# Where the weight transposes of a two-block transformer run, forward and backward on one core: DMA in the opening, TensorE between two passes

## The chip, the cores and the metric

The program runs on one core of a Trainium2 chip. The metric is the device time of one launch in microseconds (us). A core has five instruction streams that each run in order: TensorE (PE, matmuls and the transposes it can do against an identity), VectorE (DVE), ScalarE (ACT), GpSimd (POOL) and SyncE (SP). Here DMAs are issued from two of these streams, SP and ACT; their data move on 16 DMA engines that the two share.

## The reference, cut to what matters

Four layers A, B, A, B on x of 2048 x 640, with weights shared between the two A layers and between the two B layers, and then all gradients. Heads: 32 of width 20.

```python
x = x + A(layernorm(x))   # linear attention
x = x + B(layernorm(x))   # softmax attention over a window of 256
x = x + A(layernorm(x))
x = x + B(layernorm(x))
# A: q, k, v = h @ wqkv; phi(t) = where(t > 0, t + 1, exp(t)) + 1e-6
#    kv = sum_s phi(k) v;  z = sum_s phi(k);  o = phi(q) kv / (phi(q) z);  return o @ wo
# B: o = softmax(mask(q k^T / sqrt(20))) v;  return o @ wo
out, vjp = jax.vjp(f, A_x, A_wqkv, A_wo, B_wqkv, B_wo)
return (out, *vjp(grad_out))
```

The backward pass multiplies by the transposed weights, so each of the four weight matrices is needed once as it is and once transposed. Those four transposes are what the change moves.

## The kernel before, in words

x is cut into 16 tiles of 128 rows (TT = 16), the width into 5 blocks of 128 (DT = 5). `forward` runs four stages one after the other, and the stages overlap only at their seams.

1. The opening: `a_first` for layer 0. Per tile: `ln` (lines 469 to 484: two BATCH_NORM_STATS2 and the aggregate on DVE, two small activations on ACT for the reciprocal root, one DVE operation that writes `hn`), a transpose of `hn` on PE with an ACT copy, a store of `hn` from SP (line 484), and six chunks of q, k, v (`a_qkv`, five matmuls of 320 columns each), with their exponentials on ACT and their maxima on DVE; ACT issues five stores per tile. `hn` has one buffer (`hnA`, line 372), so the `hn` of a tile waits until the store of the tile before has landed.
2. Pass 0 (`ab_pass(0)`): for each tile the second half of layer 0 (`a_num`, `out_proj`), all of layer 1 (`ln`, `b_qkv`, `attn`, `out_proj`) and the first half of layer 2.
3. Between the passes: the key-value sums of layer 2 (`a_kv(2)`) and six tiles of late queries (`late_q`), which are fillers for PE.
4. Pass 2: the second half of layer 2, all of layer 3, and the first steps of the backward pass.

After `forward` come four backward stages, which read the transposed weights from DRAM (`WqTA`, `WoTA`, `WqTB`, `WoTB`).

What sets the order inside `forward` is a planner (`Sched`, line 87). Every step is recorded as an `Op` with an engine, a duration or a DMA size, and the buffers it reads and writes. `Sched.order` (line 126) then plays the program through with its own costs (lines 164 to 178), always taking the operation that can start first, and the instructions are emitted in that order; each engine executes its own in order. In the planner's book a DMA transpose ("T") holds SP for about 1.26 us and a shared channel for 1.17 us per 160 KB; a plain DMA ("D") holds SP for 0.33 us. A filler is taken only if nothing else can start within 300 ns (line 160). The planner's dependencies shape the order only; the waits in the program come from the buffers that the instructions touch. The framework also gives each DMA, from SP or ACT alike, one of eight completion counters in turn (they show as DMAHW0 to DMAHW7 among the waits in the built program), and an issue waits until the DMA that had the counter before has landed.

Weight transposes before the change:

- `wflips` (line 906): 20 pairs, spread by `wf` and `ws` (line 958) over pass 0. Each pair is a DMA transpose of a 128 x 640 block of `Wqkv_A` (15) or `Wo_A` (5) from SBUF into a `pp` buffer (two of them), issued by SP, and a store of that buffer to `WqTA` or `WoTA`, also from SP.
- `bflips` (line 919): 15 such pairs between the passes, from `B_wqkv` in DRAM into `KT`, `QT` and `e` buffers and out to `WqTB`.
- `early_dO` (line 712): at the start of pass 2, five DMA transposes of `Wo_B` into `WoTB` (which lies over `vv`, so after the last reader of layer 2's v), and one store.

Loads and zeroing before: lines 936 to 938 issue x in three parts (tile 0; tiles 1 to 3; tiles 4 to 15). Lines 1041 to 1044 load `Wo_A`, `Wqkv_B` and `Wo_B` in 15 pieces; they name ("vv", tt, 5) as what they follow, which at that point of the recording has no writer yet, so that they follow nothing. Lines 1039 to 1040 put 14 memsets on DVE that zero `mbd` and the q, k, v slabs of layer 1; they have no predecessor either. In PSUM the score banks of `attn` (`s3`, three banks, and `s1`) are the tiles `singles`.

Of the kernel before, what the change touches and what calls it, by code (L numbers as in the profile page):

```python
# [86 lines left out]
class Sched:  # L87
# [38 lines left out]
    def order(self):  # L126
# [23 lines left out]
        while len(out) < len(self.ops):  # L150
# [16 lines left out]
            if o.dma:  # L167
                kind, size = o.dma
                if kind == "T":
# [31 lines left out]
class Kern:  # L201
# [130 lines left out]
    def forward(self, slabs):  # L332
# [5 lines left out]
        with ExitStack() as st:  # L338
# [130 lines left out]
            def ln(l, tt, hn, hnT, how):  # L469
# [14 lines left out]
                dma("SP", lambda: self.tm_view(self.hn_d[l])[:, tt, :], lambda: hn.t, 160 * KB, [hn], [])  # L484
# [421 lines left out]
            def wflips(i, gate):  # L906
                def f():
                    et, part = divmod(i, 4)
                    key, dst, n, a = ("Wqkv_A", "WqTA", self.QTT, part * DT) if part < 3 else ("Wo_A", "WoTA", DT, 0)
                    c0 = part * D if part < 3 else 0  # L910
                    b = R["pp"].buf()
                    keys = [("Wqkv_A", i) for i in range(6)] if part < 3 else [key]
                    view = lambda: b.t.rearrange("p (k q) -> p k q", k=DT)
                    flip(view, lambda: wsb[key][:, et, c0:c0 + D], 160 * KB, keys + [gate], [b])
                    dma("SP", lambda: W[dst].rearrange("p (a b) -> p a b", a=n)[:, a:a + DT, et * P:(et + 1) * P],
                        view, 160 * KB, [b], [])
                return f

            def bflips(i, gate):
                def f():  # L920
                    et, part = divmod(i, 3)
                    kind = ("KT", "QT", "KT", "e", "e")[i % 5]
                    b = R[kind].buf()
                    view = lambda: (b.t[:, 0:DT, :] if kind != "e" else
                                    b.t.rearrange("p h i q -> p (h i) q")[:, 0:DT, :])
                    flip(view, lambda: self.B_wqkv[et * P:(et + 1) * P, part * D:(part + 1) * D], 160 * KB, [gate], [b])
                    dma("SP", lambda: W["WqTB"].rearrange("p (a b) -> p a b", a=self.QTT)[
                        :, part * DT:(part + 1) * DT, et * P:(et + 1) * P], view, 160 * KB, [b], [])
                return f
# [28 lines left out]
            AT = {0: dict(wf=-2.296, ws=0.65, num=-2.458, out=-1.707, outb=1.792, step=0.144, qkv=-0.99, wide=0.745, lag=0.42, af=2.042, al=-0.11),  # L958
                  2: dict(lq=-3.207, num=-2.403, out=-1.76, outb=1.696, step=0.086, qkv=-0.985, wide=0.584, lag=0.35, gT=0.745, dO=1.691, dOs=0.137)}

            def ab_pass(l, last):
# [75 lines left out]
            a_first(items, 0, 0)  # L1037
            spread(items, 1.0, 9.0, [lambda f=f: op("POOL", 350, f, [], ["masks"]) for f in self.mask_steps])
            spread(items, 2.0, 12.0, [lambda t=t, v=v, n=n: op("DVE", 100 + n * 0.45, lambda: nc.vector.memset(t, v), [],
                                                               ["zeros"]) for t, v, n in zeros])  # L1040
# [7 lines left out]
            for i in range(3 * DT):  # L1048
                bflips(i, ("rs", 1, TT - 1))()
            for tt in range(EARLY):  # L1050
# [3 lines left out]
                        for o in S.rd.get(k, ())}  # L1054
            a_users = {o for i in range(6) for o in S.rd.get(("Wqkv_A", i), ())}
# [812 lines left out]
```

## Time and profile before

| what | us |
|---|---|
| device time, median of 3 runs (lowest, highest) | 2163.03 (2159.4, 2163.52) |
| the profiled execution's own device time | 2163.08 |
| its span, first to last instruction | 2161.4 |
| the opening, to the last transpose of `pqT` | 0 to about 113 |
| pass 0, first product with `mbd` to the last scores | about 118 to 418 |
| between the passes, to the second product with `mbd` | about 418 to 452 |
| mean granted TensorE clock | 0.973 |

How to read the lines: in a timeline the columns are start, duration, engine, line, operation, out<-in, how many were merged, and in brackets how long the engine had been idle and what released it. SPq and ACTq are DMA issues on these streams. In a view of stretches each engine has its busy time and its number of instructions, then the granted PE clock (1.00 is full), the busy share of the 16 DMA engines and GB/s. In a list of DMA issues the last two columns are KB of one and the median us from issue to landing. Matmul ends are modelled, so a group's start-to-start distance says more than its duration.

### The profile page before, as it was taken

Reading aid. Unit: us, or ns where it says so; the run is one execution under the profiler, and the core shown is the slowest. Engines: PE = TensorE matmul, PEld = TensorE weight load, DVE = VectorE, ACT = ScalarE, POOL = GpSimd, SP = SyncE. Lnnn points to the kernel's source line nnn. Section 1 sums busy time; section 2 is a strip of 40 time slices with the busy share of each in tenths; the row PEclk is TensorE's granted clock in tenths of the full one; section 3 lists DMA queues with packets and bytes.
Section 4 is the critical chain, followed back from the end, with each engine's and each line's share of the span. In section 5 each row is a group of like instructions: output and inputs, shape, how many; then the busy total and the mean of one; then the engine's idle time right before and its main releaser. Section 6 shows DMA issues by size and latency. Waiting matters only on the chain. (4 is left out here: it accounts for less than half of the span.)

```text
span 2161.4 us, 67833 instructions
## 1 busy us (share of the span) xinstructions
PE 2008.5 (93%) x27808; PEld 1384.3 (64%) x27808; DVE 1441.9 (67%) x2954; ACT 1191.9 (55%) x1975; POOL 879.2 (41%) x1850
## 2 busy tenths in 40 slices
PE   6878899879999899999899999998999999999999
PEld 4645666556666567777666667655777765666764
DVE  7656677567777489999734459605999984444651
ACT  4617778617888589899522223215889882121430
POOL 1015566506777556666323213203656651221210
PEclk9979999999999989999999999998999989999999
DMA  7449998788999688988997899836998997989843
GB/s 274 171 136 194 191 199 185 173 220 182 211 210 199 144 157 157 159 155 151 200 187 168 208 196 214 181 95 143 154 159 151 166 169 162 195 181 230 186 112 102
DMA packets 964808, 379.70 MB, mean 176 GB/s; under 512 B 844817, under 2 KB 944785, under 8 KB 964241
## 3 DMA queue, kind: packets, MB, share of 16 engines
q1 hardware_dynamic: 887296, 302.44, 72.5%
q10 hardware_dynamic: 77200, 72.94, 10.9%
q8 instruction: 217, 3.56, 0.7%
q14 instruction: 95, 0.77, 0.1%
HBM read 109.02 MB, written 112.07 MB: 102 GB/s over the span
## 5 line engine op out<-in xcount | busy, mean ns | idle before, releaser
L1668 DVE TENSOR_TENSOR ds_sb<-pair,e_sb 128x768 bf16<-128x768 f32 x480 | 438.0, 952 | 58.4 <-PE pair L1629 50.9
L1648 ACT ACTIVATE e_sb<-pair 128x768 bf16<-128x768 f32 x480 | 391.0, 815 | 95.6 <-PE pair L1629 66.3
L841 POOL TENSOR_SCALAR_AFFINE_SELECT e_sb<-e_sb 128x384 bf16<-128x384 bf16 (+1 forms) x512 | 198.2, 406 | 373.7 <-ACT e_sb L832 347.3
L832 ACT ACTIVATE e_sb<-s_ps 128x1152 bf16<-128x1152 f32 (+2 forms) x256 | 273.9, 1070 | 107.0 <-PE s_ps L828 71.0
L1660 POOL TENSOR_SCALAR_AFFINE_SELECT e_sb<-e_sb 128x256 bf16<-128x256 bf16 x448 | 182.1, 407 | 226.9 <-ACT e_sb L1648 226.8
L1302 POOL TENSOR_TENSOR gw<-w,gcar 128x640 f32<-128x640 f32 x64 | 89.4, 1398 | 423.9 <-ACT w L1299 400.4
L1113 PEld LDWEIGHTS <-slabR 128*128 128x128 bf16 x1920 | 185.7, 98 | 116.2 <-DMA slabR<-o 5.8
L1657 POOL TENSOR_SCALAR_AFFINE_SELECT e_sb<-e_sb 128x256 bf16<-128x256 bf16 x512 | 206.5, 406 | 90.1 <-ACT e_sb L1648 90.1
L1693 PEld LDWEIGHTS <-dsT 128*128 128x128 bf16 x2880 | 146.3, 97 | 96.7 <-issue 90.4
L1684 ACT COPY dsT<-dsT_ps 128x768 bf16<-128x768 bf16 x240 | 191.2, 797 | 10.2 <-PE dsT_ps L1681 7.3
L446 PE MATMUL mm_ps<-slabR,hnTB 128*128 128x320 bf16 x960 | 170.5, 309 | 8.4 <-DVE gcar L518 6.1
L1681 PE MATMUL dsT_ps<-ident,ds_sb 128*128 128x128 bf16 x1848 | 158.4, 223 | 1.6 <-ACT dsT L1684 1.1
L1697 PEld LDWEIGHTS <-e_sb 128*128 128x128 bf16 x2880 | 145.2, 96 | 0.0
L1697 PEld LDWEIGHTS <-ds_sb 128*128 128x128 bf16 x2880 | 145.1, 96 | 0.0
L846 POOL TENSOR_SCALAR_AFFINE_SELECT e_sb<-e_sb 128x512 bf16<-128x512 bf16 x224 | 142.5, 636 | 0.0
L835 ACT ACTIVATE e_sb<-s_ps 128x384 bf16<-128x384 f32 (+2 forms) x256 | 119.8, 468 | 36.6 <-PE s_ps L828 10.1
L1113 PE MATMUL dw_ps<-dqkv,slabR 128*128 128x480 bf16 x640 | 134.6, 366 | 0.0
L1113 PE MATMUL dw_ps<-dqkv,om 128*128 128x480 bf16 x640 | 134.2, 366 | 0.0
L1284 ACT ACTIVATE dh<-mm_ps 128x320 f32<-128x320 f32 x64 | 28.0, 437 | 191.6 <-PE mm_ps L1113 153.3
L1629 PE MATMUL pair<-slabR 32*128 32x384 bf16 (+2 forms) x1024 | 121.6, 329 | 11.5 <-DVE ds_sb L1668 5.0
L866 PE MATMUL pv_ps<-v_slab,e_sb 128*128 128x32 bf16 x2880 | 117.7, 177 | 12.9 <-POOL e_sb L846 10.7
L866 PEld LDWEIGHTS <-e_sb 128*128 128x128 bf16 x2880 | 106.0, 96 | 35.6 <-POOL e_sb L846 14.6
(227 smaller groups left out, 4299.3 us busy)
## 6 DMA issues: line engine op xcount, KB each, us to landing
qkvp<-qk_slab SPq DMA_DIRECT2D x64, 256.0 KB, 3.4
hn<-slabR SPq DMA_DIRECT2D x64, 160.0 KB, 3.0
qkvp<-v_slab SPq DMA_DIRECT2D x32, 256.0 KB, 3.5
slabR<-qkvp SPq DMA_DIRECT2D x16, 512.0 KB, 5.2
o<-o SPq DMA_DIRECT2D x48, 160.0 KB, 2.8
eq<-ee ACTq DMA_DIRECT2D x32, 160.0 KB, 3.0
pq<-pp ACTq DMA_DIRECT2D x32, 160.0 KB, 2.0
ek<-ee ACTq DMA_DIRECT2D x32, 160.0 KB, 2.3
```

Of the source, the lines that this page charges most:

```text
L446: nc.tensor.matmul(ps.t[:, w0:w0 + width], lhsT=lhsT(), rhs=rhs(), start=start, stop=stop)
L832: op("ACT", av(3 * nkt * P), lambda: nc.scalar.activation(e.t[:, 0:3, 0:nkt, :], s3.t[:, :, 0:nkt * P].rearrange("p h (i q) -> p h i q", q=P),
L841: nc.gpsimd.affine_select(out=v, in_=v, compare_op=ALU.is_ge, fill=0.0, base=0, pattern=[[0, h1 - h0], [1, P]], channel_multiplier=-1)
L866: nc.tensor.matmul(pv.t[:, h % 16, :], lhsT=e.t[:, hh, j, :], rhs=vts[j].t[:, h, :], start=(j == 0), stop=(j == nkt - 1))
L1113: nc.tensor.matmul(ps.t[:, w0:w0 + width], lhsT=lhsT(), rhs=rhs(), start=start, stop=stop)
L1648: nc.scalar.activation(E[n][:, 2 * p:2 * p + 2], PR[h][:, :, 0:3 * P].rearrange("p i (j q) -> p i j q", q=P), ACT.Exp, scale=self.c_att)
L1657: nc.gpsimd.affine_select(out=e[:, :, j, :], in_=e[:, :, j, :], compare_op=ALU.is_ge, fill=0.0, base=0, pattern=[[0, 2], [-1, P]], channel ...
L1660: nc.gpsimd.affine_select(out=e[:, :, j, :], in_=e[:, :, j, :], compare_op=ALU.is_ge, fill=0.0, base=-1, pattern=[[0, 2], [1, P]], channel ...
L1668: nc.vector.tensor_mul(DS[n][:, hs], PR.pop(h)[:, :, 0:3 * P].rearrange("p i (j q) -> p i j q", q=P), E[n][:, hs])
L1681: nc.tensor.transpose(ps[:, i, j, :], DS[n][:, 2 * p + i, j, :], self.ident)
L1684: (nc.scalar.copy if by == "A" else nc.vector.tensor_copy)(TSB[h], TPS.pop(h))
L1697: nc.tensor.matmul(a[:, 1 + x, hh, :], lhsT=src[n][:, hh, j, :], rhs=ld[g][rhs][:, q, cs], start=(i == 0), stop=(i == len(dkv) - 1))
```

## The change

It does five things.

1. The 20 `wflips` leave pass 0 and the 15 `bflips` leave the seam. In their place `flip_w` records 20 pairs in the opening: DMA transposes from DRAM of `B_wqkv` (15) and `A_wo` (5) into `KT` and `e` buffers, with a store each to `WqTB` or `WoTA`; pair i is placed at tile 4.5 + i/2 of the opening and planned behind the reciprocal root of the tile before that.
2. `turn_w` transposes `Wqkv_A` (15 groups) and `Wo_B` (5 groups) between the passes on PE, as fillers: five 128 x 128 transposes per group into one score bank, one ACT copy out, and for `Wqkv_A` one store from SP. The groups of `Wo_B` copy into `WoTB` behind the last readers of layer 2's k and v. All of these operations are added to the users of the last `s3` buffer, so the first scores of pass 2 come after them. The five DMA transposes of `early_dO` go; its store stays.
3. x tiles 4 to 15 are loaded behind the first `hn` store on SP, and the 15 pieces of the other weights behind the `hn` stores of tiles 1 to 15 (key ("hnd", 0, tt), which has a writer).
4. The 14 memsets are planned behind the reciprocal roots of tiles 3 to 12.
5. The planner has two new kinds of DMA cost: "L" for the opening's loads, with a landing time written in, and "B" for the pairs of `flip_w`.

In the built program the order of instructions differs from the opening on, on every engine.

```diff
+                if kind == "L":
+                    free[e], chan_ = t + 500, size - 2000
+                elif kind == "B":
+                    free[e], chan_ = t + 1300, t + 2500
+                elif kind == "T":
                     free[e] = t + 1100 + size / 1000
                     chan = max(chan, t + 800) + size / 140
...
-                o.end = chan + 2000
+                o.end = (chan_ if kind in "BL" else chan) + 2000
...
-                dma("SP", lambda: self.tm_view(self.hn_d[l])[:, tt, :], lambda: hn.t, 160 * KB, [hn], [])
+                dma("SP", lambda: self.tm_view(self.hn_d[l])[:, tt, :], lambda: hn.t, 160 * KB, [hn], [("hnd", l, tt)])
...
             def early_dO():
-                for et in range(DT):
-                    flip(lambda et=et: WoTB[:, :, et * P:(et + 1) * P], lambda et=et: wsb["Wo_B"][:, et, :], 160 * KB,
-                         ["Wo_B", ("rs", 3, 0)], [("WoTB", et)])
-                    after_kv(S.ops[-1])
...
+            def turn_w(name, n, keys, dst, done, after=()):
+                F = dict(filler=True)
+                for q in range(n):
+                    ps = R["sb"].buf()
+                    ps.make = lambda ps=ps: singles[ps.idx % 3].bitcast(BF).rearrange("p (k q) -> p k q", q=P)
+                    def f(ps=ps, q=q):
+                        for et in range(DT):
+                            nc.tensor.transpose(ps.t[:, et, :], wsb[name][:, et, q * P:(q + 1) * P], self.ident)
+                    o = op("PE", pe([P] * DT), f, keys, [ps], **F)
+                    o.deps.update(o_ for o_ in R["s3"].items[-1].ops if not o_.filler)
+                    turned.append(o)
+                    out, key = dst(q)
+                    turned.append(op("ACT", av(D), lambda ps=ps, out=out: nc.scalar.copy(out(), ps.t[:, 0:DT, :]), [ps],
+                                     [key], **F))
+                    turned[-1].deps.update(after)
+                    turned[-1].deps.discard(turned[-1])
+                    done(q, out, key)
+            def flip_w(i, gate):
+                def f():
+                    et, part = divmod(i, 4)
+                    src, name, n, a = ((self.B_wqkv, "WqTB", self.QTT, part * DT) if part < 3 else (self.A_wo, "WoTA", DT, 0))
+                    c0 = part * D if part < 3 else 0
+                    kind = ("KT", "e")[i % 2]
+                    b = R[kind].buf()
+                    view = lambda: (b.t if kind == "KT" else b.t.rearrange("p h i q -> p (h i) q"))[:, 0:DT, :]
+                    flip(view, lambda: src[et * P:(et + 1) * P, c0:c0 + D], 160 * KB, [gate], [b])
+                    S.ops[-1].dma = ("B", 0)
+                    dma("SP", lambda: W[name].rearrange("p (a b) -> p a b", a=n)[:, a:a + DT, et * P:(et + 1) * P],
+                        view, 160 * KB, [b], [])
+                    S.ops[-1].dma = ("B", 0)
+                return f
...
-            for t0, t1 in ((0, 1), (1, 4), (4, TT)):
-                dma("SP", lambda t0=t0, t1=t1: x[:, t0:t1, :], lambda t0=t0, t1=t1: xin[:, t0:t1, :],
-                    160 * (t1 - t0) * KB, [("Wqkv_A", 0)] if t0 == 4 else [], [("x", i) for i in range(t0, t1)])
+            def load_x(t0, t1, lands):
+                dma("SP", lambda: x[:, t0:t1, :], lambda: xin[:, t0:t1, :], 160 * (t1 - t0) * KB,
+                    [("hnd", 0, 0)] if t0 >= 4 else [], [("x", i) for i in range(t0, t1)])
+                S.ops[-1].dma = ("L", lands)
+            load_x(0, 1, 2800)
+            load_x(1, 4, 5500)
...
-                    for i in range(4 * DT):
-                        t = min(int(a["wf"] + a["ws"] * i), TT - 1)
-                        items.append((t + 0.05, len(items), wflips(i, ("rs", 1, t))))
...
+            items.append((0.5, len(items), lambda: load_x(4, TT, 14000)))
-            spread(items, 2.0, 12.0, [lambda t=t, v=v, n=n: op("DVE", 100 + n * 0.45, lambda: nc.vector.memset(t, v), [],
-                                                               ["zeros"]) for t, v, n in zeros])
+            spread(items, 3.0, 13.0, [lambda t=t, v=v, n=n, i=i: op(
+                "DVE", 100 + n * 0.45, lambda: nc.vector.memset(t, v), [("rs", 0, 3 + i * 10 // len(zeros))], ["zeros"])
+                for i, (t, v, n) in enumerate(zeros)])
...
-                    items.append((tt + 0.9, len(items), lambda k=k, src=src, j=j, tt=tt: load_w(k, src, "SP", j, [("vv", tt, 5)])))
+                    items.append((tt + 0.9, len(items), lambda k=k, src=src, j=j, tt=tt: load_w(k, src, "SP", j, [("hnd", 0, tt)])))
+            for i in range(4 * DT):
+                at = 4.5 + 0.5 * i
+                items.append((at, len(items), flip_w(i, ("rs", 0, int(at) - 1))))
...
-            for i in range(3 * DT):
-                bflips(i, ("rs", 1, TT - 1))()
...
+            turn_w("Wqkv_A", self.QTT, [("Wqkv_A", i) for i in range(6)], *staged("WqTA", self.QTT))
+            turn_w("Wo_B", DT, ["Wo_B"], lambda q: (lambda: WoTB[:, q, :].rearrange("p (k q) -> p k q", q=P), ("WoTB", q)),
+                   lambda q, out, key: None, kv_users)
+            R["s3"].items[-1].ops.extend(turned)
```

More of the change, by code (lines that the diff above doesn't have):

```diff
@@ L168, in order @@
                 kind, size = o.dma
-                if kind == "T":
+                if kind == "L":
[3 more added lines that the diff above has]
+                elif kind == "T":
                     free[e] = t + 1100 + size / 1000
@@ L907, in f @@
+            def flip_w(i, gate):
                 def f():
                     et, part = divmod(i, 4)
-                    key, dst, n, a = ("Wqkv_A", "WqTA", self.QTT, part * DT) if part < 3 else ("Wo_A", "WoTA", DT, 0)
+                    src, name, n, a = ((self.B_wqkv, "WqTB", self.QTT, part * DT) if part < 3 else (self.A_wo, "WoTA", DT, 0))
                     c0 = part * D if part < 3 else 0
-                    b = R["pp"].buf()
-                    keys = [("Wqkv_A", i) for i in range(6)] if part < 3 else [key]
@@ L916, in f @@
+                    S.ops[-1].dma = ("B", 0)
+                    dma("SP", lambda: W[name].rearrange("p (a b) -> p a b", a=n)[:, a:a + DT, et * P:(et + 1) * P],
                         view, 160 * KB, [b], [])
+                    S.ops[-1].dma = ("B", 0)
                 return f
[L919 to L922, printed above, removed]
-                    b = R[kind].buf()
[L924 to L929, printed above, removed]
+            turned = []
@@ new lines, in forward, with staged, dst, done @@
+            R["sb"] = Ring(3, tiles=singles[0:3], name="sb")
+            def staged(W_, n):
+                def dst(q):
+                    kind = ("KT", "e")[len(turned) // 2 % 2]
+                    b = R[kind].buf()
+                    return (lambda: b.t[:, 0:DT, :] if kind == "KT" else
+                            b.t.rearrange("p h i q -> p (h i) q")[:, 0:DT, :]), b
+                def done(q, out, b):
+                    dma("SP", lambda: W[W_].rearrange("p (a b) -> p a b", a=n)[:, q, :].rearrange("p (k q) -> p k q", q=P),
+                        out, 160 * KB, [b], [])
+                return dst, done
```

7 lines of the change are left out of this document (2 added, 5 removed).

## Prediction, made before the changed kernel was run

> **What bounds the kernel.** I read the page first, then the waits, then stretches of the timeline. PE is busy nearly all the time, so a change to the other queues pays only where PE has holes.
>
> ```profile
> PE 2008.5 (93%) x27808; PEld 1384.3 (64%) x27808; DVE 1441.9 (67%) x2954; ACT 1191.9 (55%) x1975; POOL 879.2 (41%) x1850
> ...
> 0.00:20.00 20.00, 6.14 (x25) 3.24 (x25) 13.88 (x38) 4.34 (x10) 5.89 (x26) 1.00 0.95 334
> 40.00:60.00 20.00, 17.53 (x155) 12.81 (x155) 15.62 (x46) 12.37 (x31) 0.00 (x0) 1.00 0.46 162
> 424.00:452.00 28.00, 22.09 (x265) 16.64 (x264) 15.46 (x46) 4.11 (x11) 0.08 (x1) 0.88 0.96 219
> 452.00:481.00 29.00, 21.70 (x196) 14.21 (x194) 22.57 (x57) 4.52 (x13) 0.00 (x0) 1.00 0.94 236
> 186.35:318.41 132.06, 115.96 (x1883) 80.21 (x1882) 89.55 (x220) 93.47 (x153) 75.43 (x166) 0.94 0.93 190
> 318.41:384.06 65.65, 62.39 (x1076) 44.11 (x1075) 50.46 (x126) 53.48 (x89) 43.91 (x96) 1.00 0.89 195
> ```
>
> The holes: the first 20 us (6.14 busy), pass 0 up to 318 us, and the seam at 424 to 481 us. After 318 us pass 0 is at 95%. The change touches each of the three holes. The backward pass follows in series, so what the forward part gains or loses stays to the end.
>
> **The start: loads and zeroing.**
>
> ```profile
> x<-in_A_x_dram SPq DMA_DIRECT2D x1, 160.0 KB, 2.8
> ...
> hn<-slabR SPq DMA_DIRECT2D x1, 160.0 KB, 9.6
> ...
> 5.66 2.11 DVE L1039 MEMSET v_slab<- 128x512 uint32 x4
> 7.69 0.82 DVE L474 BATCH_NORM_STATS2 st<-x 128x6 f32<-128x320 bf16 x2
> 9.35 0.45 DVE L480 TENSOR_SCALAR slabR<-x,mv,rs 128x640 bf16<-128x640 bf16 x1
> ...
> 19.82 0.43 DVE L480 TENSOR_SCALAR slabR<-x,mv,rs 128x640 bf16<-128x640 bf16 x1
> ...
> 11.35 1.52 PE L446 MATMUL s_ps<-Wqkv_A,hnTA 128*128 128x320 bf16 x5 [0.78 <-ACT hnTA L465]
> 12.66 4.12 PE L446 MATMUL mm_ps<-Wqkv_A,hnTA 128*128 128x320 bf16 x15
> 20.31 0.71 PE L462 MATMUL s_ps<-ident,slabR 128*128 128x128 bf16 x5 [3.52 <-DVE slabR L480]
> ```
>
> x tile 0, issued at 0.8 us, lands after 2.8, at 3.6; its statistics start at 7.69 because the memsets stand ahead of them on DVE. Without these: statistics at 3.65, and the same steps as before put the first chunk at 11.35 - 4.04 = 7.3 us. The second delay is the larger one. The first hn store takes 9.6 us to land, since all loads are ahead of it on SP's queue, and the single hn buffer makes tile 1 wait until 19.82. In the changed program only x tiles 0 to 3 stand ahead of that store. It is issued at about 5.9 and lands between 7.8 (plus 1.9, the landing in the quiet opening, below) and some 10.8 (the 3.1 MB then asked for, from 1.5 on at the 334 GB/s of the first 20 us); I take 9.5. Two chunks of tile 0 at 1.31 and 1.37 (12.66 - 11.35, 4.12 / 3) run to 10.1, tile 1's transposes and copy take to 11.5, its first two chunks to 14.3. By then four chunks and tile 1's transposes are done, which before stood at 20.8. **Gain 6.5**, bounds 4 and 8.
>
> The load of x tiles 4 to 15 now waits for the first hn; behind it on SP is only tile 1's hn store. It has 1.6 MB of weights less ahead of it than before, and tile 4 is needed only after tiles 1 to 3. The later weight pieces I cost at nothing: pass 0 reads them from about 118 us on, the last goes out with tile 11, near 78 (14.3 + 11 x 5.77, the pace below); without these 40 us a late piece would stop PE for its landing, some 4 us.
>
> The memsets don't vanish; they now fall between evictions.
>
> ```profile
> L1039 DVE MEMSET v_slab<- x10: 112/298/485, 5.7 to 10.1; 128x512 uint32 x5, 128x64 bf16 x5
> L1039 DVE MEMSET qk_slab<- x3: 485/485/485, 4.0 to 5.1; 128x512 uint32 x3
> L1039 DVE MEMSET mbd<- x1: 1658/1658/1658, 2.3 to 2.3; 128x1920 uint32 x1
> ```
>
> 1.66 + 8 x 0.485 + 5 x 0.11 = 6.1 us. DVE is 78% busy there (15.62 of 20), so the bounds are 0 and 6.1. The longest falls at tile 1, between two k evictions for which PE's kv sums wait. **Loss 3**, half.
>
> **Twenty pairs leave pass 0.** This is the largest term.
>
> ```profile
> L418 SPq DMA_TRANSPOSE hnTB<-slabR x8: 1200/1254/1617, 186.4 to 318.4; - x8
> L418 SPq DMA_TRANSPOSE hnTB<-slabR x5: 1236/1240/1246, 318.4 to 384.1; - x5
> ...
> L414 SPq DMA_DIRECT2D WoTA<-pp x5: 546/559/785, 134.2 to 305.1; - x5
> ...
> pp<-Wqkv_A SPq DMA_TRANSPOSE x7, 3.6
> ...
> pp<-slabR SPq DMA_TRANSPOSE x3, 4.1
> ...
> 246.90 0.49 ACT L835 ACTIVATE e_sb<-s_ps 128x384 bf16<-128x384 f32 x1 [3.52 <-DMA pp<-slabR]
> 248.40 0.49 PE L866 MATMUL pv_ps<-v_slab,e_sb 128*128 128x32 bf16 x12 [2.99 <-POOL e_sb L846]
> ...
> PE pv_ps L866 <- POOL e_sb L846: 7.3, 7, 3.0
> ```
>
> The hnTB transpose comes once per tile. Eight starts span 132.06 us: seven tiles of 18.87. The last five span 65.65: four tiles of 16.41. The tiles do the same work (same blocks per head from tile 2 on); what ends at 305.1 are the pairs. The stretch 186 to 318 held ten (7 + 3), and the last rows show how they hurt: an ACT exponential waits 3.52 us for a pp transpose to land although it does not use it, since ACT's own stores queue for a completion counter that the transpose still holds; POOL's mask and PE's values follow. **Gain** 7 x (18.87 - 16.41) = **17.2**, or 1.72 per pair. Bounds: 0 if those tiles are slow for another reason; 20 x 1.72 = 34 if the ten earlier pairs cost as much. No clean stretch shows that for tiles 0 to 3, so I give them nothing.
>
> **The same number of pairs enters the opening.** There they add 40 DMAs to a queue that has seven per tile.
>
> ```profile
> 57.46 0.33 ACTq L414 DMA_DIRECT2D eq<-ee  x1
> 74.78 0.33 ACTq L414 DMA_DIRECT2D eq<-ee  x1
> ek<-ee ACTq DMA_DIRECT2D x12, 160.0 KB, 1.8
> hn<-slabR SPq DMA_DIRECT2D x11, 160.0 KB, 1.9
> ...
> 428.48 0.44 ACT L514 ACTIVATE ee<-mm_ps 128x320 bf16<-128x320 f32 x1 [5.11 <-DMA linv<-slabR]
> 439.67 0.44 ACT L514 ACTIVATE ee<-mm_ps 128x320 bf16<-128x320 f32 x1 [5.81 <-DMA hn<-slabR]
> 413.22 0.85 PE L446 MATMUL mm_ps<-Wqkv_A,pqT 128*128 128x320 bf16 x5 [1.45 <-DMA pqT<-slabR]
> 440.96 2.83 PE L446 MATMUL mm_ps<-Wqkv_A,pqT 128*128 128x320 bf16 x10 [3.36 <-DVE gcar L518]
> KT<-in_B_wqkv_dram SPq DMA_TRANSPOSE x6, 4.2
> ```
>
> A tile of the opening takes 5.77 us (three tiles from 57.46 to 74.78). It will issue 11 DMAs instead of 7, so the eighth one before an issue is some 4.2 us old. Stores land in 1.8 us and hold nobody up; a transpose from DRAM that lands in 4.2 is at the edge. Behind a waiting store on ACT stand the q, k exponentials, for which DVE and PE wait; behind a waiting store on SP stands the next hn store, for which the next hn waits. Price: at least 0 (DMA share only 0.46 there), at most 1.72 per pair, 34. Nearest are the 15 pairs of the seam, the same transposes from DRAM: PE lost 1.45 + 3.36 = 4.8, or 0.32 per pair. I take that: **loss 6.4**.
>
> **The seam.** The 15 pairs go, and with them that 4.8. In come 100 transposes and 20 ACT copies.
>
> ```profile
> 45.41 0.44 PE L462 MATMUL s_ps<-ident,slabR 128*128 128x128 bf16 x5
> 45.69 0.71 PE L446 MATMUL s_ps<-Wqkv_A,hnTA 128*128 128x320 bf16 x4
> ...
> L465 ACT COPY hnTA<-s_ps 128x640 bf16<-128x640 bf16 x12 | 8.3, 690 | 2.5 <-DVE mv L476 1.4 <-DVE pp L518 1.0
> ```
>
> Five take 0.28 us of PE from start to start (0.71 at the low clock of the start), so 20 groups take 5.6, and the copies 20 x 0.69 = 13.8 of an ACT that is busy 4.11 of 28 and 4.52 of 29. PE has 13.2 us of holes from 424 to 481. But a filler also lands in front of chain work, and pass 2's first scores wait for all of them: bounds 0 and 14.2 (20 x 0.71). I take half of 5.6, so 4.8 - 2.8, a **net gain of 2.0**. [...]
>
> The five transposes out of pass 2's start: 0. PE never waited for them; the late queries ran meanwhile. Without that cover they would be worth their own 0.32 each.
>
> **Sum** against the profiled execution's own 2163.1 (span 2161.4 and 1.7 around it; the median is the same within 0.1): -6.5 + 3.0 - 17.2 + 6.4 - 2.0 = -16.3, so **2147**. Own range 2139 to 2159: the start's and the memsets' bounds, and pairs at half to twice 0.32.
>
> **Rivals.**
> The stall moves along: the opening's pairs cost what pass 0's did, 34.4. For it: ACT's dense stores and one hn buffer. Against: stores land in 1.8 us there, DMA share half. Sum 2175, slower; it decides once a pair costs over 1.13 us (22.7 / 20). Chance 0.10.
> The slow tiles are not the pairs' doing, but the planner's early order: no 17.2, so 2164. For it: the waits of the values add up to only 7.3 us. Against: the pace changes right after the last pair. 0.10.
> The transposes on PE stretch the seam by 14.2 and the old stalls stay: -6.5 + 3 - 17.2 + 6.4 + 14.2 = 0, so 2163. Against: PE's holes. 0.08.
> Only the waits go, not the clock: 186 to 318 ran at 0.94 against 1.00, 0.06 x 132 = 7.9 us of the 17.2. If the clock has another cause, 2155. Against: it recovers as the waits end. [...] 0.07.
> The opening hides pairs and memsets: 2147 - 9.4 = 2138. For it: DMA at 0.46, SP mostly waiting. 0.15.
> The forecast: 0.50.
>
> **Numbers.** The range runs from 2133 (the hidden opening with the start's 8 and two of the ten earlier pairs at 1.72) to 2164 (the two cases of no gain); it leaves out the slow rival and the tails. Within 0.2%, 4.3 us, this measurement can't tell a change. Faster: forecast 0.50, hidden opening 0.15, clock 0.07, and 0.06 from the two cases at zero: 0.78. Same 0.08, from these two. Slower 0.14: the first rival and the rest of these.
>
> **What would show it.** First PE chunk near 7.3 us and tile 1's hn near 9.5, not 19.8. hnTB transposes 16.4 us apart from tile 4 on, no ACT wait named after a weight transpose in pass 0, clock 1.00 there. Opening tiles at about 6.4 us (5.77 + 9.4 / 15); at 7.5 or more with ACT waiting for DMAs the first rival holds. At the seam, no ACT wait of 5 us. A pass 0 still at 18.9 per tile would sink the forecast.

## The result, and the profile after

The changed kernel takes 2150.18 us (median of 20 runs; 2143.38 to 2155.26), the kernel before 2158.82 beside it (20 runs; 2148.88 to 2168.42). The ratio of the means, 2150.18 to 2159.69, is 0.9956, with a 95% interval of 0.9943 to 0.9969: **9.5 us faster**, between 6.7 and 12.3. The profiled execution of the changed kernel has a span of 2153.2; it is the slowest of the 20.

How long each engine was busy in stretches of the changed kernel (columns as in the prediction's stretches):

```profile
0.00:20.00 20.00, 10.47 (x60) 6.42 (x61) 9.40 (x26) 7.29 (x18) 5.97 (x26) 0.91 0.87 305
40.00:60.00 20.00, 15.05 (x122) 10.60 (x120) 12.96 (x38) 9.35 (x23) 0.00 (x0) 0.86 0.99 252
187.68:323.63 135.95, 127.79 (x2182) 89.17 (x2180) 102.27 (x256) 108.60 (x177) 88.44 (x194) 0.99 0.87 185
323.63:373.28 49.65, 47.41 (x820) 33.41 (x819) 38.38 (x95) 40.85 (x68) 32.92 (x72) 1.00 0.91 194
418.00:446.00 28.00, 24.89 (x338) 19.96 (x335) 19.18 (x58) 12.22 (x26) 0.00 (x0) 1.00 0.57 189
446.00:475.00 29.00, 23.15 (x218) 15.60 (x216) 20.29 (x49) 10.55 (x26) 4.64 (x12) 0.87 0.74 192
```

The row from 187.68 to 323.63 holds eight tiles of pass 0, the row before the change (186.35 to 318.41) seven. Two of the three holes are smaller: PE is busy 10.5 of the first 20 us (6.1 before), and pass 0 runs at 94% with the clock at 0.99 (88% and 0.94). A new hole is the opening, with 15.05 busy at 40 to 60 us (17.53) and the DMA engines full, 0.99 (0.46).

To see where the time goes, follow two marks through both traces: the transposes of a tile's `hn` in the opening (PE), and the `hnTB` transposes of the passes (SP; the row gives the first and the last start). First the kernel before, then the changed one:

```profile
102.19 0.44 PE L462 MATMUL s_ps<-ident,slabR 128*128 128x128 bf16 x5
...
L418 SPq DMA_TRANSPOSE hnTB<-slabR x13: 1200/1240/1617, 171.0 to 384.1; - x13
L418 SPq DMA_TRANSPOSE hnTB<-slabR x13: 1200/1277/1737, 501.8 to 695.1; - x13
```

```profile
7.16 1.51 PE L450 MATMUL s_ps<-Wqkv_A,hnTA 128*128 128x320 bf16 x5 [0.79 <-ACT hnTA L469]
...
12.33 0.45 PE L466 MATMUL s_ps<-ident,slabR 128*128 128x128 bf16 x5 [2.33 <-DVE slabR L484]
...
108.42 0.44 PE L466 MATMUL s_ps<-ident,slabR 128*128 128x128 bf16 x5 [0.84 <-ACT vv L503]
...
L422 SPq DMA_TRANSPOSE hnTB<-slabR x13: 1206/1245/1802, 174.0 to 373.3; - x13
L422 SPq DMA_TRANSPOSE hnTB<-slabR x13: 1229/1281/1567, 490.6 to 683.8; - x13
```

| mark | before | after | difference |
|---|---|---|---|
| tile 1's `hn` transposes, opening | 20.31 | 12.33 | -8.0 |
| tile 15's `hn` transposes, opening | 102.19 | 108.42 | +6.2 |
| `hnTB` of tile 3, pass 0 | 171.0 | 174.0 | +3.0 |
| `hnTB` of tile 15, pass 0 | 384.1 | 373.3 | -10.8 |
| `hnTB` of tile 3, pass 2 | 501.8 | 490.6 | -11.2 |
| `hnTB` of tile 15, pass 2 | 695.1 | 683.8 | -11.3 |
| end of the span | 2161.4 | 2153.2 | -8.2 |

So the start gives 8.0, the opening takes 14.2 back by its last tile, pass 0 gives 13.8 and the stretch before it 3.2, the seam 0.4, pass 2 nothing. The backward part, the same program in both, is 3.1 longer here. From pass 2's last mark to the end the kernels below took between 1465 and 1481 us, so one execution can't carry a difference of 3 there.

Which DMAs ACT waits for in the opening, from 20 to 110 us (us in total, times, longest), in the kernel before and in the changed one, and how the stores of the changed one land (KB, median us to landing):

```profile
ACT vv L499 <- DMA ek<-ee: 1.9, 1, 1.9
```

```profile
ACT vv L503 <- DMA WqTB<-KT: 3.6, 1, 3.6
...
ACT vv L503 <- DMA eq<-ee: 2.4, 1, 2.4
...
ACT ee L518 <- DMA WqTB<-KT: 1.6, 2, 1.3
ACT ee L518 <- DMA KT<-in_B_wqkv_dram: 1.6, 1, 1.6
```

```profile
eq<-ee ACTq DMA_DIRECT2D x12, 160.0 KB, 3.1
ek<-ee ACTq DMA_DIRECT2D x12, 160.0 KB, 3.7
...
hn<-slabR SPq DMA_DIRECT2D x12, 160.0 KB, 3.1
```

ACT waits 9.2 us (3.6 + 2.4 + 1.6 + 1.6) for DMAs that its next operation does not use, against 2.5 before the change (the 1.9 above and 0.6 for an `hn` store); stores that landed in 1.8 to 1.9 us now take 3.1 to 3.7. It is the picture that pass 0 showed before.

### The profile page after: what moved, and what is told of

Read it like the earlier page. It is cut to its first block, busy times and chain, and to the rows that moved or that the text cites. A ratio compares the mean times of both kernels' runs of the same rounds, so it can differ in the third digit from the quotient of the medians.

```text
span 2153.2 us, 68035 instructions
## 1 busy us (share of the span) xinstructions
PE 2014.5 (94%) x27908; PEld 1391.4 (65%) x27908; DVE 1438.0 (67%) x2954; ACT 1203.7 (56%) x1995; POOL 879.4 (41%) x1850
## 3 DMA queue, kind: packets, MB, share of 16 engines
q10 hardware_dynamic: 77200, 72.94, 11.3%
## 5 line engine op out<-in xcount | busy, mean ns | idle before, releaser
L1147 PEld LDWEIGHTS <-slabR 128*128 128x128 bf16 x1920 | 186.2, 98 | 117.3 <-DMA slabR<-o 4.5
L1147 PEld LDWEIGHTS <-om 128*128 128x128 bf16 x800 | 77.3, 98 | 71.5 <-DMA om<-o 2.8
```

Source lines behind the costliest of these rows:

```text
L1147: nc.tensor.matmul(ps.t[:, w0:w0 + width], lhsT=lhsT(), rhs=rhs(), start=start, stop=stop)
```

## The experiments

**Theory**: the 20 pairs slow the opening. **Rivals**: the memsets, the weight loads behind the `hn` stores, the planner's new order. If it is the pairs: through the number of DMAs on the eight completion counters, through the slow transposes (medians of 3.6 to 4.5 us to landing), or through the bytes. All marks are of one profiled execution each. Results of all (tile 15: `hn` transposes; pass 0 and seam: `hnTB` marks of the profiled execution):

| kernel | tile 15 | pass 0, tile 3 | pass 0, 3 to 15 | seam | ratio to before (95%) |
|---|---|---|---|---|---|
| before | 102.2 | 171.0 | 213.1 | 117.7 | 1 |
| after | 108.4 | 174.0 | 199.3 | 117.3 | 0.9956 (0.9943 to 0.9969) |
| e1 pairs early in pass 0 | 98.5 | 166.7 | 205.3 | 114.3 | 0.9952 (0.9931 to 0.9972) |
| e2 pairs spread over pass 0 | 99.0 | 166.2 | 214.0 | 118.3 | 0.9986 (0.9963 to 1.0009) |
| e3 memsets on POOL | 115.1 | 177.1 | 196.3 | 117.0 | 0.9992 (0.9971 to 1.0012) |
| e4 start alone | 98.5 | 164.1 | 210.7 | 117.1 | 0.9981 (0.9964 to 0.9998) |
| e5 plain loads | 106.8 | 170.7 | 195.8 | 115.7 | one run (2143.38 us) |
| e6 pair stores from POOL | 108.1 | 173.5 | 196.1 | 115.9 | 0.9971 (0.9956 to 0.9986) |
| e7 memsets in tiles 1, 2 | 103.7 | 172.0 | 202.5 | 118.2 | 0.9962 (0.9949 to 0.9976) |
| e9 all on PE | 98.7 | 165.6 | 195.5 | 141.2 | 1.0047 (1.0029 to 1.0064) |
| e10 thin pairs | 100.3 | 172.7 | 196.1 | 115.8 | one run (2157.97 us) |
| e12 weight loads early | 109.4 | 173.1 | 195.7 | 115.4 | 0.9927 (0.9899 to 0.9956) |
| e13 pairs later | 103.3 | 175.2 | 197.1 | 115.4 | 0.9960 (0.9940 to 0.9981) |
| e14 12 pairs and 8 | 104.3 | 168.8 | 197.0 | 119.2 | 0.9950 (0.9930 to 0.9971) |

**e1 and e2: the pairs in pass 0 again.** Both take buffers from `pp`, as before the change; e2 with 0.65 and e1 with 0.35 tiles from pair to pair.

```diff
-            for i in range(4 * DT):
-                at = 4.5 + 0.5 * i
-                items.append((at, len(items), flip_w(i, ("rs", 0, int(at) - 1))))
...
+                    for i in range(4 * DT):
+                        t = min(int(-2.3 + 0.35 * i), TT - 1)   # e2: -2.296 + 0.65 * i
+                        items.append((t + 0.05, len(items), flip_w(i, ("rs", 1, t))))
```

> The 20 pairs stand in tiles -2 to 4 of pass 0 instead of the opening. If the pairs are what slowed the opening (theory), tile 15's hn transposes start near 95 us instead of 108.4 (before's 102.2 less the start's 8), and the time is 2150 - 13 = 2137 plus what the pairs cost in their new place: 0 if that stretch, whose DMA share is 0.23 to 0.29, hides them, so 2137; at 0.69 per pair (13.8 / 20, what pass 0 gave back) 2151. If the memsets or the weight loads slowed the opening (rival), tile 15 stays near 106 to 108 and the time is 2150 or more.

> The 20 pairs stand spread over pass 0 as before the change, everything else as changed. Theory: tile 15 of the opening near 95 us, hnTB transposes of pass 0 again 18.9 us apart up to the last pair (213 us from tile 3 to tile 15 instead of 199), so 2150 - 13 + 14 = 2151. Rival (the slow tiles of pass 0 came from the planner's order of the old kernel and not from pairs): they stay 16.5 us apart and the time is 2137.

Without pairs the opening's tile 15 comes at 98.5 and 99.0, also in e4 and e9 (98.5, 98.7), instead of 108.4: the opening pays **9.4 to 9.9 us for 20 pairs**, 0.49 each. Both expectations put tile 15 near 95, as if the start's 8.0 us lasted; e4 shows that 3.7 of them reach tile 15. In e2 pass 0 takes 214.0 again; in the nine kernels with no pair in these tiles it takes 195.5 to 199.3. Over the stretch that the prediction measured, e2 reads:

```profile
180.57:313.98 133.41, 117.17 (x1898) 80.55 (x1897) 90.46 (x223) 94.31 (x155) 76.80 (x168) 0.94 0.92 191
313.98:380.28 66.30, 63.01 (x1082) 44.56 (x1079) 51.16 (x127) 54.17 (x89) 43.83 (x96) 1.00 0.92 190
```

Seven tiles of 19.06 (133.41 / 7) up to the last pair and four of 16.58 after it, as in the kernel before: the slow tiles and their clock of 0.94 come and go with the pairs. e2's profiled execution is the slowest of its ten (2176.97, median 2160.40), so the clean tiles of the same execution are what its slow tiles compare with. The intervals of e1, e2 and the changed kernel overlap, so the times alone do not tell the three apart; what e1 wins in the opening (9.9) it pays back in pass 0 (its tile 15 is at 372.0, 1.3 ahead of the changed kernel's).

**e3 and e7: the memsets elsewhere.** e3 puts them on POOL; e7, built on e1, at tiles 1 and 2.

```diff
-                "DVE", 100 + n * 0.45, lambda: nc.vector.memset(t, v), [("rs", 0, 3 + i * 10 // len(zeros))], ["zeros"])
+                "POOL", 100 + n * 0.9, lambda: nc.gpsimd.memset(t, v), [("rs", 0, 3 + i * 10 // len(zeros))], ["zeros"])
...
+                    "DVE", 100 + n * 0.45, lambda: nc.vector.memset(t, v), [("hnd", 0, 0) if i < 2 else ("rs", 0, 2)], ["zeros"])))   # e7
```

> The 14 memsets go to POOL, which is idle in the opening, in place of DVE. If they cost what the forecast took, 3 us, the time is 2147; if the whole 6.1 us of DVE lie on the path, 2144, with tile 15 of the opening at 102. If the pairs alone slowed the opening, tile 15 stays within 1 us of 108.4 and the time at 2150.

> The kernel with the pairs early in pass 0, and the 14 memsets moved to tiles 1 and 2 of the opening, where DVE waits 2.9 and 2.7 us for a DMA, instead of tiles 3 to 12. The clean opening gained 8.0 us at tile 1 but only 3.6 at tile 15. If the memsets took the 4.4 in between, tile 15 comes at 94 to 96 instead of 98.5 and the time falls by 3 to 4 below that kernel's 0.9952 of before, to about 0.9935. If the 4.4 come from the loads (x tiles 4 to 15 and the weight pieces between the hn stores), tile 15 stays at 98 to 99.

Both expectations failed. In e3 tile 15 comes 6.7 later, and the timeline of DVE and POOL shows the loss in one row:

```profile
7.68 3.30 POOL L1068 MEMSET mbd<- 128x3840 bf16 x1
8.70 0.89 DVE L478 BATCH_NORM_STATS2 st<-x 128x6 f32<-128x320 bf16 x2 [2.80 <-DMA x<-in_A_x_dram]
...
10.91 2.74 POOL L1068 MEMSET qk_slab<- 128x1024 bf16 x3
11.84 6.90 DVE L484 TENSOR_SCALAR slabR<-x,mv,rs 128x640 bf16<-128x640 bf16 x1 [1.26 <-DMA hn<-slabR]
13.60 4.96 POOL L1068 MEMSET v_slab<- 128x1024 bf16 x10
18.66 0.22 DVE L519 TENSOR_SCALAR ee<-ee 128x320 bf16<-128x320 bf16 x1
```

Tile 1's `hn`, 0.45 us elsewhere, takes 6.90 beside POOL's memsets. So e3 says nothing of their price on DVE. In e7 DVE's holes were no holes: two memsets stand ahead of tile 1's `hn` and twelve ahead of tile 3's, and tile 15 comes 5.1 later than in e1. In the changed kernel the memset of `mbd` (1.66 us) stands ahead of the `gcar` for which PE then waits 1.8 us; what the other 13 cost was not separated from the start's gain.

**e4: the start alone**, on the kernel before: its loads, its keys and its memsets as changed, all weight transposes as before.

```diff
-                    160 * (t1 - t0) * KB, [("Wqkv_A", 0)] if t0 == 4 else [], [("x", i) for i in range(t0, t1)])
+                    [("hnd", 0, 0)] if t0 >= 4 else [], [("x", i) for i in range(t0, t1)])
...
-... load_w(k, src, "SP", j, [("vv", tt, 5)])))
+... load_w(k, src, "SP", j, [("hnd", 0, tt)])))
```

> The kernel before with the start's edits alone (loads behind the first hn store, weight pieces behind the hn stores, memsets behind the roots), all weight transposes where they were. Forecast: -6.5 + 3.0, so 2155.3 against 2158.8. If the memsets and the weight loads cost nothing in the opening and the pairs all: -8.0, tile 15 of the opening at 94, 2151. If the memsets cost 6.1 there: tile 15 at 100 and 2157.

0.9981, that is 4.1 us (0.4 to 7.8), and tile 15 at 98.5 instead of 102.2: start and memsets together give 3.7, where the forecast had 3.5.

**e5, e6 and e10: why a pair costs 0.49.** In all three PE, DVE and ACT run the opening in the order of the changed kernel. e5 replaces the transposes by plain loads; e6 issues the pairs' stores from POOL; e10 keeps each pair as two plain DMAs of 16 of the 128 rows.

```diff
-                    flip(view, lambda: src[et * P:(et + 1) * P, c0:c0 + D], 160 * KB, [gate], [b])   # e5
+                    dma("SP", view, lambda: src[et * P:(et + 1) * P, c0:c0 + D].rearrange("p (k q) -> p k q", q=P), 160 * KB, [gate], [b])
...
-                    dma("SP", lambda: W[name].rearrange("p (a b) -> p a b", a=n)[:, a:a + DT, et * P:(et + 1) * P],   # e6
+                    dma("POOL", lambda: W[name].rearrange("p (a b) -> p a b", a=n)[:, a:a + DT, et * P:(et + 1) * P],
...
-                    flip(view, lambda: src[et * P:(et + 1) * P, c0:c0 + D], 160 * KB, [gate], [b])   # e10
+                    dma("SP", lambda: view()[0:16], lambda: src[et * P:et * P + 16, c0:c0 + D].rearrange("p (k q) -> p k q", q=P), 160 * KB, [gate], [b])
```

> The changed kernel with the opening's 20 DMA transposes replaced by plain loads of the same blocks (the two transposed weights then hold untransposed blocks); number, order and issuing engines of all DMAs are the same. If the opening slows because of how many DMAs share the eight completion counters, its tile 15 stays near 108 us. If it slows because transposes occupy the DMA engines and land late (3.6 to 4.5 us), plain loads land in about 2 us and tile 15 comes back to 98.5 to 101, as in the kernels without pairs in the opening; DMA share of 20 to 100 us falls from 0.96 to 1.00 to some 0.75.

> The changed kernel with the stores of the opening's 20 pairs issued from POOL, which is idle there, so that only the 20 transposes are left on the counters that SP and ACT share. Counter theory: half or more of the 9.9 us come back, tile 15 at 100 to 103.5 and 2145 to 2150 against 2150 (or the same ratio to before). DMA engine theory: the same bytes move, tile 15 stays within 1.5 us of 108.4, the time at 2150 or, since POOL's issues cost more, a little above.

> The changed kernel with the opening's 20 pairs as plain DMAs of 16 of the 128 rows: number, order and issuing engine of all DMAs of the opening, and so the turns of the completion counters, and the order of PE, DVE and ACT are unchanged, the pairs' bytes are an eighth. (The transposed weights get untransposed data by two copies after the opening.) If the bytes on the DMA engines set the price, tile 15's hn transposes come back to 98.5 to 100 us, and stores land in about 2 us. If the number of DMAs on the eight counters or the planner's order sets it, tile 15 stays at 106 to 108.

The stretch from 20 to 100 us in the changed kernel, in e1 (no pairs there), e6, e5 and e10, one fence each:

```profile
20.00:100.00 80.00, 64.17 (x542) 45.83 (x542) 56.14 (x169) 41.63 (x102) 0.00 (x0) 0.94 0.99 261
```

```profile
20.00:100.00 80.00, 69.81 (x610) 49.88 (x610) 61.70 (x184) 47.53 (x117) 0.00 (x0) 0.98 0.66 216
```

```profile
20.00:100.00 80.00, 61.78 (x543) 44.59 (x543) 58.00 (x169) 42.13 (x102) 17.46 (x20) 0.96 1.03 273
```

```profile
20.00:100.00 80.00, 64.25 (x554) 45.53 (x554) 57.32 (x172) 42.34 (x103) 0.00 (x0) 0.96 0.89 272
```

```profile
20.00:100.00 80.00, 67.13 (x596) 48.29 (x596) 61.52 (x183) 46.17 (x114) 0.00 (x0) 1.00 0.70 218
```

Read the last two columns, then PE. With seven eighths of the pairs' bytes gone and the number and order of DMAs in place (e10), the share falls to 0.70, PE gains 3.0 us in this stretch, ACT waits for no DMA in it, and tile 15 comes at 100.3:

```profile
100.34 0.44 PE L466 MATMUL s_ps<-ident,slabR 128*128 128x128 bf16 x5 [1.24 <-ACT vv L503]
```

**What the pairs put on the DMA engines carries 8.1 of the 9.9 us**, number and order at most 1.8. e10 thins bytes and packets together (from 20 to 100 us 17.42 MB in 15425 packets, 20.89 MB in 34414 in the changed kernel) and does without the transposing; plain loads of the full bytes (e5) give back only 1.7, at a share of 0.89, so the transposes as such are a small part, and tile 15 comes at neither of the two times that e5's expectation named. (Behind tile 15 two copies fill the weights in e10, and PE waits 4.71 us for ACT ahead of 109.80; its later marks and its time say nothing here.) Taking 20 of the 40 DMAs off the counters that SP and ACT share (e6; POOL's DMAs have eight of their own, DMASW0 to DMASW7 in the built program) gives back 0.3; ACT still waits up to 6.0 us for one store:

```profile
ACT vv L503 <- DMA eq<-ee: 7.5, 2, 6.0
```

So a full counter is how the wait reaches ACT (in the built program of the changed kernel each of the 1707 DMAs is issued only after the one that had its counter before has landed), and full DMA engines are why the counter is held so long (ACT waits 9.2 us for DMAs at a share of 0.99, none at 0.70 in e10). e6 alone would not show it, since the load grew with it: the share is 1.03, and the stores from POOL land in 3.8 to 4.7 us (2.7 to 4.1 from SP in the changed kernel; medians). An issue from POOL also costs more, as the expectation says: POOL shows 17.46 us for the 20 stores, 0.87 each, against medians of 0.38 to 0.58 for SP's issues of them in the changed kernel. The theory that the number of DMAs on the counters sets the price falls with e10.

**e12: the weight loads out of the pairs' way**. In the changed kernel the 15 pieces follow the `hn` stores of tiles 1 to 11 (1 + 3i + j in the code, the last issued at 87.3 us), not of tiles 1 to 15 as the section on the change and the expectation say; so the edit makes groups of seven, seven and one behind the `hn` stores of tiles 1 to 3, not of five.

```diff
-... load_w(k, src, "SP", j, [("hnd", 0, tt)])))
+... load_w(k, src, "SP", j, [("hnd", 0, 1 + (tt - 1) // 5)])))
```

> The changed kernel with the 15 weight pieces in groups of five behind the hn stores of tiles 1 to 3, instead of one behind each of tiles 1 to 15. If the pairs are dear because the change also moved the 3.2 MB of weight loads on top of them, the later opening gets faster: from tile 7 to tile 15, 62.7 us in the changed kernel, it takes 57 or less (52 in the kernels without pairs), against which the early tiles lose up to 8; tile 15 at 102 to 110. If the weight pieces don't matter, 62 to 63 from tile 7 to 15.

The figures in it count from tile 6's transposes, not tile 7's. The rows for tile 6 of the changed kernel (its tile 15 is at 108.42, above), tiles 6 and 15 of e1, and tiles 6 and 15 of e12:

```profile
45.77 0.44 PE L466 MATMUL s_ps<-ident,slabR 128*128 128x128 bf16 x5
```

```profile
46.55 0.45 PE L466 MATMUL s_ps<-ident,slabR 128*128 128x128 bf16 x5 [0.70 <-DVE slabR L484]
...
98.54 0.44 PE L466 MATMUL s_ps<-ident,slabR 128*128 128x128 bf16 x5 [0.78 <-ACT vv L503]
```

```profile
51.83 0.45 PE L466 MATMUL s_ps<-ident,slabR 128*128 128x128 bf16 x5 [1.47 <-DVE slabR L484]
...
109.38 0.44 PE L466 MATMUL s_ps<-ident,slabR 128*128 128x128 bf16 x5
```

These nine tiles take 62.7 us in the changed kernel and 52.0 in e1. In e12 they take 57.6, just above the bound, and the tiles before lose 6.1. Only one weight piece still goes out in them (at 56.7 us). Beside the opening's stores and that piece, 14 pairs cost 5.6 us, 0.40 each; beside stores and weight loads, 15 pairs cost 10.7, 0.71 each. The loads alone cost nothing that shows: e1, which has them in these tiles, takes 52.0, and the kernel before, which has issued all of them by 32 us, 52.3 (102.19 - 49.90). The loads have to pass somewhere, so tile 15 of e12 is no earlier (109.4).

**e13 and e14: fewer pairs in the opening.** e13 places all of them five tiles later; e14 leaves 12 there and puts 8 behind the store of `mbd`, a wait that the program really makes.

```diff
-                at = 4.5 + 0.5 * i
+                at = 9.5 + 0.5 * i   # e13
...
+            for i in range(12):   # e14
+                at = 6.5 + 0.75 * i
+                items.append((at, len(items), flip_w(i, ("rs", 0, int(at) - 1))))
...
             a_kv(0)
+            for i in range(12, 4 * DT):
+                flip_w(i, ("zsel", DT - 1))()
```

> The changed kernel with the 20 pairs five tiles later, so that some eight of them run after the last hn store, in the stretch of 108 to 140 us where the DMA share was 0.23 to 0.29 and ACT is idle. If a pair costs about 0.5 us only beside the opening's stores and loads, tile 15 comes at 103 to 105, pass 0 stays clean (196 to 199 from hnTB of tile 3 to tile 15), and the time falls by 4 to 2146 (0.994 of before). If what the late pairs save comes back in pass 0's first tiles, tile 3's hnTB stays at 173 to 174 and the time at 2150.

> The changed kernel with 12 of the 20 pairs in the opening, three to every four half tiles from tile 6.5 on, and 8 behind the store of layer 0's mbd on SP, that is in the stretch of about 120 to 140 us where ACT issues next to nothing, behind a real wait. At 0.49 us per pair beside the opening's stores tile 15 comes at 98.5 + 12 x 0.49 = 104.4 (108.4 in the changed kernel); if the 8 late pairs are hidden, tile 3's hnTB of pass 0 comes at 170 instead of 174 and the time is 4 lower, a ratio to before of 0.994 (0.9956 for the changed kernel). If they only move the loss, tile 3's hnTB stays at 173 to 175 and the ratio at 0.9956 or above.

In e13 tile 15 is 5.1 earlier, and all of it is lost after that: the pairs bunch beside the last tile's stores. ACT's timeline, then PE's:

```profile
109.27 0.33 ACTq L418 DMA_DIRECT2D ek<-ee  x1
113.53 0.35 ACTq L418 DMA_DIRECT2D pk<-gcar  x1
113.92 0.43 ACT L503 CAST vv<-s_ps 128x320 bf16<-128x320 f32 x1 [4.36 <-DMA ek<-ee]
```

```profile
114.39 1.49 PE L450 MATMUL s_ps<-Wqkv_A,hnTA 128*128 128x320 bf16 x5 [4.25 <-ACT vv L503]
```

An issue that should follow at 109.6 comes at 113.5, and PE stands for 4.25 us. In e14 the trace does what was expected: tile 15 at 104.3 (104.4), tile 3's `hnTB` at 168.8 (170), the 8 late pairs hidden, and pass 0's last tile 7.5 ahead of the changed kernel. The time does not show it: 0.9950 (0.9930 to 0.9971). Likewise e6, whose marks run ahead of the changed kernel's by 5.2 at the end of pass 2, has 0.9971. Whether a shorter forward part lengthens the backward part, or profiled and timed executions differ by that much, stays open. So the 0.994 that both expectations named is neither met nor ruled out. No version is shown to beat the changed kernel; e12 has the lowest ratio, and its interval reaches 0.9956.

**e9: all four weights on PE at the seam**, two more calls behind the two that are there, and no pairs.

```diff
+            turn_w("Wqkv_B", self.QTT, ["Wqkv_B"], *staged("WqTB", self.QTT))
+            turn_w("Wo_A", DT, ["Wo_A"], *staged("WoTA", DT))
             R["s3"].items[-1].ops.extend(turned)
```

> All four weight transposes on PE between the passes: the 20 pairs leave the opening, 20 more groups of five transposes join the 20 groups there. Opening as in the kernels without pairs, tile 15 at 98.5 (gain 9.9). If a group costs its PE time of 0.28 us and the rest hides, the stretch between the passes (hnTB of pass 0's tile 15 to that of pass 2's tile 3, 117.3) grows by 5.6 to 123, net gain 4.3, 2146. If the ACT copies set the pace, 0.69 each, it grows by 13.8 to 131, net loss 3.9, 2154. If PE's holes hide the groups, 2140.

The only version slower than the kernel before, 2171.86 us. Opening and pass 0 are clean, but the seam grows by 23.9 (141.2 - 117.3), 1.2 us per added group, more than any of the three cases of the expectation:

```profile
451.70 0.69 PE L915 MATMUL s_ps<-ident,slabR 128*128 128x128 bf16 x5 [0.78 <-ACT KT L920]
452.43 0.69 ACT L920 COPY e_sb<-s_ps 128x640 bf16<-128x640 bf16 x1 [0.78 <-PE s_ps L915]
...
453.17 0.69 PE L915 MATMUL s_ps<-ident,slabR 128*128 128x128 bf16 x5 [0.78 <-ACT e_sb L920]
453.90 0.69 ACT L920 COPY KT<-s_ps 128x640 bf16<-128x640 bf16 x1 [0.78 <-PE s_ps L915]
```

With no other work left to fill, PE and ACT take turns at 1.47 us per group (453.17 - 451.70), though three score banks are in the ring. In the built program the first transpose of each of these groups waits for the copy just before it. Five transposes take 0.69 there and 0.44 in a group shortly before, at 446.92; in the kernel before they took 0.71 at a granted clock of 0.50 (20.31 us; 20 to 21.5). Holes that hide 20 groups did not hide 40.

## Why the prediction was right in direction and too high in gain

- **The start and the memsets** (6.5 - 3.0 = 3.5): right. First chunk at 7.16 (7.3 forecast), four chunks and tile 1's transposes done at about 14.6 (14.3), and the sum 3.7 in e4's marks. The order within it differs: the third and fourth chunk (12.62, 13.30) start before tile 1's copy (13.35), so they are still tile 0's, and tile 1's `hn` comes at 11.8, not 9.5. Within it one bound was too narrow, as DVE's timeline shows:

```profile
11.83 0.45 DVE L484 TENSOR_SCALAR slabR<-x,mv,rs 128x640 bf16<-128x640 bf16 x1 [1.49 <-DMA hn<-slabR]
...
17.40 0.45 DVE L484 TENSOR_SCALAR slabR<-x,mv,rs 128x640 bf16<-128x640 bf16 x1 [2.30 <-DMA hn<-slabR]
```

  The first `hn` store lands at 11.8, not between 7.8 and 10.8, and tile 2's `hn` waits for tile 1's store. The bound counted only what stood ahead of the first store; the x load of tiles 4 to 15 (1.9 MB) goes out at 6.0, 0.4 us behind it. The first wait leaves PE idle for 2.33 us ahead of tile 1's transposes; the second is hidden, since PE has chunks to run until then.
- **Pass 0** (17.2): right. Clean pass 0 takes 195.5 to 197.1 from tile 3 to 15 in eight of the experiments, 16.0 to 17.6 less than the 213.1 before, and e2 brings the slow tiles back. The changed kernel's own profile shows 13.8, because one tile of it took 19.2 at a lower clock:

```profile
237.70:254.90 17.20, 16.46 (x282) 11.60 (x279) 13.28 (x33) 13.95 (x23) 10.90 (x24) 1.00 0.91 184
254.90:274.10 19.20, 16.77 (x270) 11.32 (x268) 12.72 (x32) 13.49 (x23) 11.00 (x24) 0.91 0.88 180
274.10:290.60 16.50, 15.75 (x277) 11.11 (x274) 12.91 (x33) 13.55 (x23) 10.95 (x24) 1.00 0.82 189
```

- **The rival "only the waits go, not the clock"** is out: 0.99 and 1.00 without pairs, 0.94 again in e2. What lowers the clock is not shown. In the stretch from 254.9 to 274.1 the longest wait of PE is 2.0:

```profile
PE pv_ps L866 <- POOL e_sb L846: 2.0, 1, 2.0
```

  From 259.1 to 262.5, around this wait, PE is busy for 1.42 us at a clock of 1.00; from there to 265.9 it is busy throughout, and the clock is at 0.51:

```profile
259.10:262.50 3.40, 1.42 (x38) 1.07 (x34) 1.80 (x4) 2.57 (x5) 1.66 (x5) 1.00 0.98 254
262.50:265.90 3.40, 3.40 (x25) 1.71 (x24) 2.59 (x7) 3.01 (x6) 1.94 (x4) 0.51 0.00 0
```

- **The pairs in the opening** (6.4, or 0.32 each): this is the step that failed, in size. Measured 9.4 to 9.9, 0.49 each. The price was taken from the seam, and "DMA share only 0.46 there" was the lower bound and the case against the rival. But that share is of the kernel before, and the same change spreads the weight loads over these tiles, which the prediction cost at nothing: without any pairs the share from 20 to 100 us is already 0.66 (e1), and with them 0.99. Each of the two was costed for itself; what counts was their sum on the 16 DMA engines. e12 shows the size: the pairs of tiles 6 to 15 cost 0.40 each almost without the loads, near the 0.32 of the seam, and 0.71 each beside them.
- **The seam** (2.0): 0.4 in the changed kernel's profile; the kernels with the same code there gain up to 3.4 (114.3, e1) and lose up to 1.5 (119.2, e14), and e4, with the pairs still there, has 117.1. ACT's waits of 5.1 and 5.8 us are gone as forecast (its longest for a DMA from 418 to 482 us is 2.7), and PE has the transposes to do instead. The net is near nothing, and one execution each doesn't settle it closer. The rival in which the transposes stretch the seam by 14.2 is out for 20 groups, and e9 shows it come true for 40.
- **The first tiles of pass 0**, which the prediction gave nothing: the stretch from tile 15's `hn` to tile 3's `hnTB` went from 68.8 to 65.6. With pairs there e4 has 65.6 too and e2 67.2; without them e9 has 66.9 and e5 63.9. So it isn't shown that this 3.2 comes from the pairs that left; what it comes from stays open.

Measured terms, from the changed kernel's marks: -3.7 + 9.9 - 3.2 - 13.8 - 0.4 = -11.2 at pass 2's tile 3, against -16.3 forecast; the -9.5 of the times agrees with -11.2 within its interval. Two things make the forecast look better than its terms. The 3.2 that no term held makes up for most of what the pairs cost above 6.4. And the forecast time of 2147 is near the measured 2150.2 because the sum starts from 2163.1, while the kernel before took 2158.8 in the 20 runs beside the changed one; of the gain of 16.3 came 9.5. The stall did move along, but at 0.49 per pair and not above the 1.13 at which the rival would have decided.

## What to carry to other kernels

Transfers moved out of a crowded stretch need room in the new place after everything else the same change puts there: here the DMA share from 20 to 100 us was 0.57 before, 0.66 with the moved loads and 0.99 with the pairs as well, and a pair then cost 0.49 us. So add up the bytes per microsecond of the new stretch, all moved parts together, before taking its old DMA share as a sign of room. A wait for a completion counter looks like a matter of how many DMAs are out, but thinning the DMAs cured it here (8.1 of 9.9 us), and taking half of the pairs' DMAs off the shared counters did not (0.3). The gap in PE hid a limited amount of filler work: the first 20 groups cost no more than the 15 DMA pairs whose place they took, the next 20 cost 1.2 us each.

## What the runs showed of the hardware that was not expected

- A DVE TENSOR_SCALAR that runs beside POOL memsets took 6.90 us instead of 0.45 (e3), while BATCH_NORM_STATS2 beside the `mbd` memset took 0.89 for two, as it does without it (0.89 at 8.46 us of the changed kernel). The TENSOR_SCALAR did not get done between POOL's memsets: it ended at 18.74 (11.84 + 6.90), just behind the last of the thirteen that followed each other, at 18.56 (13.60 + 4.96, by POOL's spans). How POOL holds it back is not shown.
- The stores of the pairs from POOL (e6) land in 3.8 to 4.7 us (medians) and leave the opening as slow as in the changed kernel (tile 15 at 108.1 and 108.4): another queue did not help here, with the DMA share at 1.03.
- In e9 most groups of five transposes and one copy run in turn over three banks of one PSUM tile, since each group's first transpose waits for the copy just before it. A kernel with the banks as separate tiles was not tried.
